# Variance by tile, modulation rows through ScalarE and TensorE, and five norm groups without a shift column, in an adaLN block on one core

## The chip, the cores and the metric

The kernel runs on one NeuronCore of a Trainium2 chip. The core has a matrix engine (TensorE, "PE" in the profile, with its weight loads as "PEld"), a vector engine (VectorE, "DVE"), an engine for activations (ScalarE, "ACT"), a general engine (GpSimd, "POOL"), and a queue engine that issues transfers (SyncE, "SP"). Each engine works through its own list of instructions in order, and semaphores make one wait for another.

The metric is the time of one execution on the device in microseconds (us), as the median of several runs. The kernel before takes 201.45 us, the median of three runs that lie between 201.2 and 201.52 us.

## The reference

One block with adaptive layer norms: x is 2048 x 512 (bf16), c is one condition row, and six modulation rows of 512 are taken from it.

```python
def _layernorm(x, axis=-1, eps=1e-05):
    m = jnp.mean(x, axis=axis, keepdims=True)
    v = jnp.var(x, axis=axis, keepdims=True)
    return (x - m) / jnp.sqrt(v + eps)
...
    mod = (_silu(c) @ w_mod).reshape(c.shape[0], 6, 1, -1)
    sa, ca, ga, sb, cb, gb = (mod[:, 0].copy(), ...)
    h = _layernorm(x, axis=-1) * (1 + ca) + sa
    x = x + ga * _A_ref(h, A_wqkv, A_wo)
    h = _layernorm(x, axis=-1) * (1 + cb) + sb
    x = x + gb * _B_ref(h, B_w1, B_b1, B_w2, B_b2)
    return x
```

`_A_ref` is an attention with 32 heads of 16 in which each position sees 8 positions at distances 0, 2, ... 14 behind it. `_B_ref` takes a third layer norm of its input and then an MLP over the tokens: 2048 tokens to 1792 hidden values with a gelu, and back to 2048. So there are three layer norms, called norm 0, 1 and 2 in the code (`l`), and `n1_`, `n2_`, `h3_` in the names of the operations.

## The kernel before

**Tiles and chunks.** The 2048 positions are 16 tiles of 128 rows. Five chunks of 2, 4, 4, 4 and 2 tiles (`SIZES`) go through norm 0, the projections to queries, keys and values, the attention, the output projection, norm 1 with its modulation, and norm 2. The token MLP begins with the tiles that are ready and fills TensorE between the attention's operations; from the last chunk on it has TensorE for itself.

**Order.** Each operation is put into a graph with a name and an engine or a choice of engines. The order in which they are issued is a list written out by hand, `ORDER` (line 191). A letter behind a colon chooses the engine (`a` ScalarE, `d` VectorE, `p` GpSimd, `s` SyncE). Each engine runs its part of the list in that order. Six PSUM buffers (`ps`) and four large SBUF buffers (`big`) are given out while the list is walked through; an operation with `alloc` takes one and the operation with `frees` gives it back, so an evacuation that comes late holds back the matmul that wants its buffer. `fill` entries are matmuls without use.

**A norm's operations.** For each tile, sums or statistics; then for a group of tiles the variance, then `ln_rstd` (line 405): `rstd...`, a logarithm and an exponential on ScalarE that give the column `rs` = 1/sqrt(var + eps), and `nb...`, one small VectorE operation that gives the shift column `nb` = -mean x `rs`. `ln_norm` (line 420) normalizes each tile as x `rs` + `nb`, on ScalarE, VectorE or GpSimd. The name after `nb` and `rstd` is the norm's number counted from one, and the chunk (norm 0) or the first tile of the group (norms 1 and 2): `nb1_0` and `nb1_1` belong to the first two chunks of norm 0, `nb3_2` to the group of tiles 2 and 3 of norm 2.

**Norm 1's variance.** For tiles 0 to 13 ScalarE or VectorE leave two sums for each tile in `sums`: of x, and 512 times the sum of the squares. The operation `ln2m...` makes from them a scaled negative variance in `mv`, for a group of tiles at once: groups begin at tiles 0, 2, 4, 6, 10 and 12 and have two tiles, the one that begins at 6 has four (`GRP`). It is two VectorE operations, of which the second reads the first one's result.

**The modulation rows.** `build_mod_rows` (line 570) multiplies the row silu(c) with columns of `w_mod`, in two parts: `modrow0` makes the row ga, `modrow1` the rows sb, cb and gb. A matmul with a 32 times repeated column of silu(c) fills one quarter of the partitions, so four stand side by side. `mrows0` and `mrows1` evacuate PSUM into `mrows`, `st_row...` stores them to memory and `ld_row...` loads them spread over all partitions (`rows_bc`). In `mrows1` VectorE copies three rows and then writes 1 + cb over the second. `aff...` applies the rows to a normalized tile.

**Attention, as far as the prediction speaks of it.** For each chunk VectorE forms products of queries and keys (`qk...`, big from `q_sb`, `k_f`), TensorE adds them up in `psL` (`red...`), VectorE takes the maximum (`max...`, tile `m`), ScalarE the exponentials (`exp...`, `lsb` from `psL`); later VectorE multiplies weights and values (`pv...`, big from `a2sb`, `vD`) and TensorE adds these up (`pvacc...`). `ev...` are the evacuations of the projections.

Of the kernel before, what the change touches and what calls it, by code (L numbers as in the profile page):

```python
# [192 lines left out]
fill:40 ln1s1:a ln1s0:d ln1v1 ld_x_2_8 ln1v0 ln1s4:d ld_wqkv0 rstd1_0 ln1s2:a nb1_0 n1_1:d n1_0:p modcols1 tr0_0  # L193
ln1s5:d ln1v4 ln1v5 ln1v3 ln1v2 rstd1_1 nb1_1 ld_x_2_6 a1col n1_2:d n1_5:d ln1s8:a wsc0_3:p n1_4:d hT0_1:a hT0_3:a
n1_3:d hT0_0:a fill:20 hT0_2:a ld_wqkv1 ld_wmod0 ln1s9:d ld_x_3_10 ln1s6:d tr1_0 tr1_2 hT1_2:a ln1v6 qkv0_02 ln1v9
hT1_0:a qkv0_12 qkv0_10 ln1s7:d ln1v7 ln1v8 rstd1_2 hT1_3:d wsc1_0:a ev0_12:a modcols0 sab:a ld_x_3_12 nb1_2 n1_8:a
qkv0_00 qvb0 wsc0_0:p ev0_10:a ld_b2 ld_wo1 hT1_1:d qkv1_00 ln1s11:d ln1s10:d ln1s13:d qkv1_10:q ln1v11 ln1v10
qvb_cp0:a ev0_00:a ln1s12:a ev0_02:d qkv1_13 ld_wqkv2 qkv0_20 ln1v13 qk0_3 qk0_2 ev1_13:a qk0_0 qvb1 ln1v12 qkv0_22:q
ld_wrow0 red0_0 ev1_00:a qkv1_03:q ev1_10:a qk0_1 red0_1 red0_2 red0_3 mask qvb_cp1:a ev0_20:a ev0_22:a wsc1_2:p
halo_v1:a qk1_0 ev1_03:a wsc1_3:a qkv1_11:q ld_wmod2 wsc2_3:a modrow0 ld_b1 mrows0:a ev1_11:a ld_wrow2 qkv1_02 max0  # L200
wsc0_2:p ld_wo0 n1_7:p sub0 rstd1_3 qkv1_01 ld_wo2 exp0 qkv1_12:q wsc1_1:p esum0:q qk1_3 red1_0 ev1_01:a qk1_1
ev1_02:a biascols n1_6:p ld_wrow1 rcp0 smB0 ev1_12:a ld_x_4_14 ln1s14:a qkv1_22 qk1_2 a2_0_2:a xt6 ld_wrow3 modrow1
red1_1 a2_0_1:a n1_9:p wsc2_0:d ln1s15:a ln1v14 nb1_3 n1_11:a qkv1_23:q mrows1 qkv1_21 ev1_21:a red1_2 red1_3 xt8
ev1_23:a fill:1 n1_10:p qkv1_20 ev1_20:a ev1_22:a qkv2_13 qkv2_10 wsc0_1:p vd0_2 ev2_13:a ln1v15 vd0_1 max1 sub1
qkv2_00 exp1 a2_0_0:s a2_0_3:s pv0_1 vd0_0 pv0_0 st_row0 pv0_2 qkv2_03 esum1:q ld_wo3 pvacc0_0 vd0_3 halo_v2:p
biascols_cp:a pvacc0_1 pv0_3 pvacc0_2 pvacc0_3 ev2_10:a ev2_00:a qk2_0 n1_13:a n1_12:a ld_row0 woq_s rcp1 smB1
oev0_2:a qkv2_11 qkv2_02:q ev2_03:a qk2_3 qkv2_01:q red2_0 oev0_0:a wo0:q wsc2_1:a wsc2_2:a qkv2_12 ev2_11:a ev2_01:a
ev2_02:a ev2_12:a wo1 qkv2_21:q a2_1_1:a qkv2_22 x1_1:a ln2q1:a x1_0:a xt10 ln2q0:a qk2_1 qkv2_23 xt12 qk2_2 a2_1_0:s
halo_k3:a ln2m0 vd1_2 a2_1_2:s qkv3_12 a2_1_3:s pv1_2 rstd1_4 red2_1 nb1_4 vd1_0 st_row1 red2_2 red2_3 rstd2_0
ev2_22:a nb2_0 ev2_21:a qkv3_13:q ev3_13:a max2 vd1_3 pv1_0 n1_14:a vd1_1 pvacc1_2 n1_15:a qkv2_20:q ev2_20:a sub2  # L210
qkv3_22:q ev3_12:a pv1_1 qkv3_10 exp2 ev2_23:a halo_v3:a qkv3_20 n2_0:a oev1_2:a ev3_10:a esum2 rcp2 qkv3_00 ev3_22:a
qkv3_02:q ev3_00:a pv1_3 ev3_02:a pvacc1_0 ev3_20:a qkv3_01:q ev3_01:a qkv3_11:q xt14 ld_row1 n2_1:p vd2_3 pvacc1_1
smB2 aff0 qk3_0 vd2_1 fill:1 vd2_0 oev1_0:a oev1_1:a pvacc1_3 ev3_11:a qk3_1 qkv3_23:q oev1_3:a a2_2_2:s ln3s1:a
qkv3_03:q wo4 a2_2_1:s qk3_2 a2_2_0:s ev3_03:a ev3_23:a x1_4:a ln2q4:a wo2 x1_2:a a2_2_3:s red3_0 wo3:q x1_3:a ln2q3:a
qkv3_21:q ev3_21:a wo5 red3_1 pv2_3 x1_5:a vd2_2 qk3_3 qkv4_20:q red3_2 qkv4_22 red3_3 qkv4_12 fill:18 ln2q5:a
ld_w1_0_512 ln2q2:a ln2m2 pv2_0 pvacc2_0 vd3_0 ev4_20:a ln3s0:a ln3v0 ev4_12:a rstd2_2 ev4_22:a ln3v1 qkv4_02 oev2_0:a
ln2m4 rstd2_4 nb2_2 n2_2:a max3 sub3:q exp3 pvacc2_3 oev2_3:a qkv4_10:q pv2_2 vd3_2 esum3 nb2_4 pv2_1 vd3_1 n2_3:p
ld_w1_0_0 n2_5:a rcp3 smB3 pvacc2_2 fill:14 a2_3_0:s a2_3_1:s a2_3_3:s n2_4:a qkv4_00:q oev2_2:a rstd3_0 aff2 pvacc2_1
oev2_1:a wo6 wo9 wo7 aff4 nb3_0 ln3s2:d ev4_02:a ln3s3:a ln3v3 h3_1:p wo8 a2_3_2:s ev4_00:a ln3v2 ld_w2_0 ln3s4:d
rstd3_2 nb3_2 x1_9:a ln3s5:a h3_0:p mlp1_0_6_0:q x1_7:a ln3v4 x1_8:a h3_3:d mlp1_0_1_0 h3_2:d mlp1_0_6_2 mlp1_0_1_2  # L220
pv3_1 mlp1_0_5_0:q ln3v5 ev4_10:a ld_w1_0_896 x1_6:a mlp1_0_3_0:q mlp1_0_3_2:q ln2q7:a pvacc3_1 rstd3_4 mlp1_0_5_2:q
oev3_1:a mlp1_0_2_0:q pv3_0 mlp1_0_2_2:q nb3_4 h3_4:a mlp1_0_0_0:q mlp1_0_0_2 h3_5:a mlp1_0_0_4:q qk4_0 ln2q8:a
ln2q6:a park0_0:a ln2q9:a mlp1_0_6_4:q mlp1_0_2_4:q mlp1_0_1_4:q park0_1:a pv3_2 mlp1_0_5_4:q vd3_3 pvacc3_0 oev3_0:a
mlp1_0_3_4:q ld_w2_1 park0_2:a pv3_3 red4_0 ln2m6 pvacc3_2 oev3_2:a mlp1_0_4_0:q qk4_1 pvacc3_3 ld_w1_0_1152
mlp1_0_4_2:q mlp1_0_4_4:q rstd2_6 oev3_3:a wo12:q halo_v4:p vd4_2 vd4_3 nb2_6 n2_9:a qk4_2 n2_7:d qk4_3 wo10:qn red4_1
ld_w1_0_1408 n2_6:a vd4_1 n2_8:a aff6 red4_2 red4_3 max4 park0_3:a ln3s8:d ln3s6:d x1_12:a ln3v8 wo11 vd4_0 ln3s9:d
mlp1_0_7_0 ld_w2_3 park0_4:a ln3v6 mlp1_0_7_2 park0_5:a ln3v9 x1_11:a ln2q12:a mlp1_0_8_0 mlp1_0_8_2 park0_6:a wo13:n
ln3s7:a ln3v7 sub4 mlp1_0_10_0 mlp1_0_9_0 x1_13:d exp4 rstd3_6 nb3_6 esum4 mlp1_0_8_4 ln2q13:a ln2m12 mlp1_0_10_2
mlp1_0_10_4 mlp1_0_9_2 rcp4 mlp1_0_7_4 h3_8:d rstd2_12 mlp1_0_12_0 mlp1_0_12_2 mlp1_0_12_4 smB4 a2_4_1:a a2_4_0:s
mlp1_0_9_4 a2_4_2:s h3_9:d a2_4_3:a h3_7:d nb2_12 h3_6:p mlp1_0_7_6 ln2q11:a park0_7:a x1_10:d mlp1_0_8_6 ld_w1_0_1664  # L230
ln2q10:a park0_8:a n2_13:p mlp1_0_9_6 park0_9:a n2_12:d aff12 ln2m10 rstd2_10 mlp1_0_10_6 park0_10:a ln3s13:a pv4_2
nb2_10 ld_w1_1_0 pv4_1 mlp1_0_11_0 mlp1_0_11_2 mlp1_0_11_4 mlp1_0_12_6 pv4_0 mlp1_0_11_6 ld_w1_1_640 inj1_6:qn pv4_3
pvacc4_0 pvacc4_1 n2_11:a mlp1_0_13_0:q pvacc4_2 pvacc4_3 n2_10:a mlp1_0_13_2:q park0_11:a mlp1_0_13_4 oev4_0:a
oev4_2:a aff10 ln3s10:a wo14 inj1_3:n ln3s11:d ln3v11 x1_14 ln2s14 wo15 x1_15 mlp1_0_13_6 ln2v14 ln3s12:a ln3v10
ln2s15 rstd2_14 nb2_14 ln2v15 n2_14:d rstd3_10 aff14 rstd2_15 nb2_15 inj1_4:qn ln3v13 park0_12:a mlp1_1_3_6 park0_13:a
mlp1_1_6_6 inj1_1:n mlp1_1_1_6 n2_15:p mlp1_1_4_6 inj1_0:n mlp1_1_0_6 nb3_10 h3_10:a mlp1_1_4_10 mlp1_1_3_10 ln3s14:d
ld_w2_4 mlp1_1_0_10 ln3v14 ln3v12 rstd3_12 h3_11:a mlp1_1_6_10 inj1_5:n mlp1_1_5_6 mlp1_1_5_10 rstd3_14 mlp1_1_1_10
aff15 nb3_12 ln3s15:d ln3v15 h3_12:p nb3_14 park1_0:+ h3_13:p rstd3_15 nb3_15 inj1_2:n mlp1_1_2_6 ld_w1_1_896 h3_14:p
h3_15:a ld_w1_2_0 park1_1:+ mlp1_1_2_10 park1_2:+ mlp1_1_7_10 park1_3:+ park1_4:+ park1_5:+ mlp1_1_8_10 mlp1_1_10_10
park1_6:+ padd1_7 padd1_10 gelu10 padd1_8 mlp1_1_9_10 padd1_9 gelu9 mlp1_2_4_11 mlp1_2_4_14 mlp1_2_1_11 mlp1_2_1_14  # L240
padd2_1 padd2_4 gelu7 mlp1_2_0_11 mlp1_2_0_14 padd2_0 gelu0 mlp1_2_2_11 gelu4 gelu8 mlp1_2_2_14 ld_w1_1_1408
mlp1_2_3_11 mlp1_2_3_14 padd2_3 gelu3 ld_w1_2_640 mlp1_2_6_11 padd2_6 gelu6 padd2_2 gelu2 mlp1_2_5_11 mlp1_1_11_10
padd1_11 mlp1_2_5_14 padd2_5 gelu1 gelu11 mlp1_1_12_10 ld_w2_5 ld_w2_7 mlp1_1_13_10 gelu5 mlp2_0_0 padd1_12 gelu12
mlp2_0_0b ld_w2_2 ld_w2_9 ld_w2_13 ld_w2_11 padd1_13 gelu13 mlp2_0_0c mlp2_6_0 mlp2_4_0 gsc fin0_0 st_out0_0 fin4_0
st_out4_0 mlp2_8_0 fin8_0 mlp2_3_0 fin3_0 mlp2_2_0 fin2_0 st_out2_0 mlp2_1_0 fin1_0 mlp2_7_0 st_out3_0 fin6_0
st_out6_0 fin7_0 mlp2_10_0 fin10_0 st_out7_0 mlp2_11_0 mlp2_5_0 st_out1_0 fin5_0 st_out5_0 mlp2_14_0 fin11_0
# [829 lines left out]
```

## Time and profile before

| | |
|---|---|
| median of the runs | 201.45 us |
| runs | 201.52, 201.45, 201.2 us |
| span of the profiled execution, first to last instruction | 199.0 us |
| median less span | 2.45 us |
| granted clock of TensorE | 1.000 |
| transfers | 35.95 MB at 181 GB/s on average |

The profile shows one execution. Its own total time is not on the page, so its span is set against the median of the runs; what lies around the span is their difference.

A row of the timeline gives the start in us from the start of the span, the length, the engine, the line, the operation, the tile written and the tiles read, their shapes, and the count of merged instructions; in brackets is how long the engine had been idle, and what released it. Instructions of one engine overlap at their ends, so what an operation adds to its engine's list is read from the start of one to the start of the next, and not from its length. Nearly all instructions have the line 142, that of the helper which records them; they are told apart by their tiles. In the chain of waits each piece is what the end of the kernel hung on in that stretch.

### The profile page before, as it was taken

What the parts mean: (1) busy time and instruction counts of PE and PEld (TensorE: products, weight loads), DVE (VectorE), ACT (ScalarE), POOL (GpSimd) and SP (SyncE); (2) the same over time, 40 slices, a digit from 0 to 9 for tenths busy, and PEclk for the clock granted to TensorE, in tenths of its full rate; (3) what the DMA queues carried; (4) which work ended last, traced back from release to release, by engine and by line L of the source; (5) the groups of instructions that cost most, each with busy time, mean ns of one, the idle gap of its engine ahead of it and who ended that gap; (6) DMA issues with size and microseconds to landing.
All of it is one profiled execution on the core that took longest, in us unless ns stands there. A gap on an engine that the chain in (4) does not pass through costs nothing.

```text
span 199.0 us, 4560 instructions
## 1 busy us (share of the span) xinstructions
PE 189.6 (95%) x1812; PEld 95.0 (48%) x1830; DVE 159.8 (80%) x242; ACT 127.8 (64%) x305; POOL 18.7 (9%) x45
## 2 busy tenths in 40 slices
...
GB/s 159 334 355 356 192 284 90 156 53 245 243 203 293 245 182 158 152 151 303 55 308 243 49 209 160 163 215 229 335 231 311 85 14 53 28 51 56 171 53 53
DMA packets 53889, 35.95 MB, mean 181 GB/s; under 512 B 24428, under 2 KB 50668, under 8 KB 53868
## 3 DMA queue, kind: packets, MB, share of 16 engines
...
q10 hardware_dynamic: 1640, 0.46, 0.9%
q8 instruction: 14, 0.23, 0.5%
q14 instruction: 7, 0.06, 0.1%
...
## 4 chain that ended last, share of the span: by engine, by line
PE 69%; DVE 22%; issue 4%; DMA 2%; ACT 2%; DVEq 0%; ACTq 0%
PE psS L142 66%; DVE big L142 14%; DVE h L142 3%; PE psL L142 3%; DMA xx<-in_A_x_dram 2%; DVE st L142 2%; DVE mv L142 1%; ACT h L142 1%; DVE lsb L142 1%; DVE m L142 1%; DVE nb L142 1%; ACT lv L142 0%; DVE woq L142 0%; ACT rs L142 0%; ACT rb L142 0%
## 5 line engine op out<-in xcount | busy, mean ns | idle before, releaser
L142 PEld LDWEIGHTS <-wst 128*128 128x128 bf16 (+1 forms) x536 | 34.9, 101 | 34.1 <-issue 4.0
L142 PE MATMUL psS<-h,wst 128*128 128x512 bf16 (+1 forms) x333 | 50.3, 379 | 0.5 <-issue 0.3
L142 DVE TENSOR_TENSOR big<-q_sb,k_f 128x4096 bf16<-128x4096 bf16 (+1 forms) x20 | 36.6, 1860 | 0.4 <-ACT q_sb L142 0.4
L142 DVE TENSOR_TENSOR big<-a2sb,vD 128x4096 bf16<-128x4096 bf16 (+1 forms) x20 | 36.6, 1862 | 0.2
L142 DVE SCALAR_TENSOR_TENSOR h<-psS,bcol,rows_bc 128x512 f32<-128x512 f32 (+2 forms) x17 | 12.1, 711 | 22.1 <-PE psS L142 20.6
L142 PE MATMUL psS<-hT,w_qkv 128*32 128x512 bf16 (+3 forms) x360 | 29.7, 345 | 0.0
L142 PEld LDWEIGHTS <-w_qkv 128*32 128x32 bf16 (+1 forms) x402 | 19.4, 108 | 17.8 <-issue 4.4
L142 PE MATMUL psS<-gT,big 128*128 128x512 bf16 x110 | 24.7, 379 | 0.1
L142 PEld LDWEIGHTS <-big 128*128 128x128 bf16 x144 | 12.1, 98 | 13.8 <-DMA big<-in_w_mod_dram 0.6
L142 ACT ACTIVATE junk<-xx 128x512 bf16<-128x512 bf16 x26 | 16.4, 629 | 3.4 <-DVE xx L142 1.4
L142 PE MATMUL psS<-woq,o_sb 128*32 128x512 bf16 (+1 forms) x107 | 15.7, 379 | 0.9 <-ACT o_sb L142 0.6
L142 ACT ACTIVATE gT<-psS,bcol 128x512 bf16<-128x512 f32 x14 | 9.0, 686 | 8.1 <-DVE psS L142 8.0
L142 POOL TENSOR_SCALAR h<-xx,rs,nb 128x512 bf16<-128x512 bf16 x9 | 7.1, 785 | 73.3 <-DVE nb L142 34.4
L142 DVE TENSOR_TENSOR psS<-psS,gT 128x512 f32<-128x512 f32 x14 | 9.3, 696 | 5.0 <-PE psS L142 5.0
L142 PE MATMUL psS<-hT,wst 128*32 128x512 bf16 (+2 forms) x110 | 12.0, 352 | 0.1
L142 ACT ACTIVATE h<-xx,nb,rs 128x512 bf16<-128x512 bf16 x15 | 11.6, 809 | 0.3 <-DVE nb L142 0.2
L142 DVE TENSOR_TENSOR h<-h,xx 128x512 bf16<-128x512 f32 (+2 forms) x17 | 11.1, 652 | 0.6
L142 DVE BATCH_NORM_STATS2 st<-xx 128x6 f32<-128x512 bf16 x12 | 8.0, 683 | 4.3 <-DMA xx<-in_A_x_dram 4.0
L142 DVE TENSOR_TENSOR h<-h,rows_bc 128x1024 bf16<-128x1024 bf16 (+2 forms) x16 | 11.0, 690 | 0.4
L142 ACT ACTIVATE v_sb<-psS,qvb 128x512 bf16<-128x512 f32 (+1 forms) x20 | 11.0, 595 | 0.0
L142 ACT ACTIVATE q_sb<-psS,qvb 128x512 bf16<-128x512 f32 (+1 forms) x18 | 10.4, 614 | 0.3 <-PE psS L142 0.3
L142 PEld LDWEIGHTS <-ident 128*32 128x32 bf16 (+1 forms) x131 | 6.2, 101 | 9.0 <-issue 4.5
...
## 6 DMA issues: line engine op xcount, KB each, us to landing
...
```

What stands on the lines that cost most here:

```text
L142: r = fn(*a, **k)
```

## The change

It has three parts, and the list `ORDER` is the same but for what they force.

1. `ln2m`: one scalar-tensor-tensor operation for each tile, (sum x sum) - 512 x (sum of squares), instead of two tensor-tensor operations for the group.
2. `mrows1`: the 1 in 1 + cb is added in PSUM by four more matmuls in `modrow1`, with a column of ones against the identity; the evacuation is then one plain copy of 384 columns, on ScalarE, at the same place of the list. GpSimd sets the column of ones at the start.
3. `NONB`: for five groups (`1_0`, `1_1`, `3_2`, `3_12`, `3_14`) there is no `nb` operation. Their tiles are normalized as (x - mean) x `rs`, which VectorE and GpSimd do with two columns as before; none of them is normalized on ScalarE in either kernel.

```diff
+    NONB=("1_0", "1_1", "3_2", "3_12", "3_14"),
...
+    ones = T([P, 1], BF, "ones")
...
         add("act", 0.54, fa, reads=reads + ["ident", "act_table"], writes=[("rs", l, g0)], name="rstd" + name)
+        if name in NONB:
+            return
...
-        G.add_any([("act", 0.8, lambda: nc.scalar.activation(dst, src, ACT.Identity, scale=r_, bias=n_)),
-                   ("dve", 0.42, lambda: nc.vector.tensor_scalar(dst, src, r_, n_, op0=ALU.mult, op1=ALU.add)),
-                   ("pool", 0.8, lambda: nc.gpsimd.tensor_scalar(dst, src, r_, n_, op0=ALU.mult, op1=ALU.add))],
-                  reads=reads + [("rs", l, g0), ("nb", l, g0)], writes=writes, name=name, locks=True)
+        sv, so = ((r_, n_), (ALU.mult, ALU.add))
+        nonb = f"{l + 1}_{g0 if l else T0.index(g0)}" in NONB
+        if nonb:
+            sv, so = (ln_t["mv", l][:, st, 0:1], r_), (ALU.subtract, ALU.mult)
+        G.add_any(([] if nonb else [("act", 0.8, lambda: nc.scalar.activation(dst, src, ACT.Identity, scale=r_, bias=n_))]) +
+                  [("dve", 0.42, lambda: nc.vector.tensor_scalar(dst, src, *sv, op0=so[0], op1=so[1])),
+                   ("pool", 0.8, lambda: nc.gpsimd.tensor_scalar(dst, src, *sv, op0=so[0], op1=so[1]))],
...
+        nc.gpsimd.memset(ones[:], 1.0)
...
-                                             rhs=w_[:, kt, dt_ * P:(dt_ + 1) * P], start=(kt == 0), stop=(kt == KT - 1),
+                                             rhs=w_[:, kt, dt_ * P:(dt_ + 1) * P], start=(kt == 0),
+                                             stop=(kt == KT - 1 and (r0, r) != (1, 1)),
                                              tile_position=(0, 32 * dt_))
+                    if (r0, r) == (1, 1):
+                        for dt_ in range(KT):
+                            nc.tensor.matmul(ps(s_)[32 * dt_:32 * dt_ + 32, r * P:(r + 1) * P],
+                                             lhsT=ones[:, 0:1].to_broadcast([P, 32]), rhs=ident[:], start=False, stop=True,
+                                             tile_position=(0, 32 * dt_))
...
-            if nr == 1:
-                copy2(rows, src_, P, False, [], [("mrows", b_)], f"mrows{b_}", frees=s_)
-            else:
-                def f_cp(rows=rows, src_=src_):
-                    nc.vector.tensor_copy(rows, src_())
-                    nc.vector.tensor_scalar_add(rows[:, 1, :], src_()[:, 1, :], 1.0)
-                add("dve", 0.8, f_cp, writes=[("mrows", b_)], frees=s_, name=f"mrows{b_}")
+            copy2(rows, src_, nr * P, False, [], [("mrows", b_)], f"mrows{b_}", frees=s_)
...
-                    gs = slice(g0, g0 + gn)
-                    if gn == 1:
-                        nc.vector.scalar_tensor_tensor(mv[:, g0, 1:2], sums[:, g0, 0:1], sums[:, g0, 0:1], sums[:, g0, 1:2],
+                    for st in range(g0, g0 + gn):
+                        nc.vector.scalar_tensor_tensor(mv[:, st, 1:2], sums[:, st, 0:1], sums[:, st, 0:1], sums[:, st, 1:2],
                                                        op0=ALU.mult, op1=ALU.subtract)
-                        return
-                    nc.vector.tensor_tensor(mv[:, gs, 0], sums[:, gs, 0], sums[:, gs, 0], op=ALU.mult)
-                    nc.vector.tensor_tensor(mv[:, gs, 1], mv[:, gs, 0], sums[:, gs, 1], op=ALU.subtract)
```

In `ORDER` the five `nb` entries are left out and `mrows1` becomes `mrows1:a`.

More of the change, by code (lines that the diff above doesn't have):

```diff
@@ L192 @@
 ident ld_x_1_2:a halo0 ld_c consts ld_x1:s ld_x0:s ld_x_1_4:s act_table ln1s3:d fill:4 cps ld_wmod1 silu_exp silu_dve
[L193 to L246, printed above, removed]
@@ L247 @@
-st_out10_0 st_out11_0 ld_w2_15 fpre mlp2_9_0 mlp2_13_0 fin14_0 st_out14_0 st_out8_0 mlp2_12_0 fin9_0 st_out9_0 fin13_0
-st_out13_0 mlp2_15_0 fin12_0 st_out12_0 fin15_0 st_out15_0 mlp2_15_1 fin15_1 st_out15_1 mlp2_15_2 fin15_2 st_out15_2
+fill:40 ln1s1:a ln1s0:d ln1v1 ld_x_2_8 ln1v0 ln1s4:d ld_wqkv0 rstd1_0 ln1s2:a n1_1:d n1_0:p modcols1 tr0_0 ln1s5:d
+ln1v4 ln1v5 ln1v3 ln1v2 rstd1_1 ld_x_2_6 a1col n1_2:d n1_5:d ln1s8:a wsc0_3:p n1_4:d hT0_1:a hT0_3:a n1_3:d hT0_0:a
+fill:20 hT0_2:a ld_wqkv1 ld_wmod0 ln1s9:d ld_x_3_10 ln1s6:d tr1_0 tr1_2 hT1_2:a ln1v6 qkv0_02 ln1v9 hT1_0:a qkv0_12
@@ new lines @@
+n1_7:p sub0 rstd1_3 qkv1_01 ld_wo2 exp0 qkv1_12:q wsc1_1:p esum0:q qk1_3 red1_0 ev1_01:a qk1_1 ev1_02:a biascols n1_6:p
+ld_wrow1 rcp0 smB0 ev1_12:a ld_x_4_14 ln1s14:a qkv1_22 qk1_2 a2_0_2:a xt6 ld_wrow3 modrow1 red1_1 a2_0_1:a n1_9:p
+wsc2_0:d ln1s15:a ln1v14 nb1_3 n1_11:a qkv1_23:q mrows1:a qkv1_21 ev1_21:a red1_2 red1_3 xt8 ev1_23:a fill:1 n1_10:p
+qkv1_20 ev1_20:a ev1_22:a qkv2_13 qkv2_10 wsc0_1:p vd0_2 ev2_13:a ln1v15 vd0_1 max1 sub1 qkv2_00 exp1 a2_0_0:s a2_0_3:s
+pv0_1 vd0_0 pv0_0 st_row0 pv0_2 qkv2_03 esum1:q ld_wo3 pvacc0_0 vd0_3 halo_v2:p biascols_cp:a pvacc0_1 pv0_3 pvacc0_2
@@ new lines @@
+halo_v3:a qkv3_20 n2_0:a oev1_2:a ev3_10:a esum2 rcp2 qkv3_00 ev3_22:a qkv3_02:q ev3_00:a pv1_3 ev3_02:a pvacc1_0
+ev3_20:a qkv3_01:q ev3_01:a qkv3_11:q xt14 ld_row1 n2_1:p vd2_3 pvacc1_1 smB2 aff0 qk3_0 vd2_1 fill:1 vd2_0 oev1_0:a
+oev1_1:a pvacc1_3 ev3_11:a qk3_1 qkv3_23:q oev1_3:a a2_2_2:s ln3s1:a qkv3_03:q wo4 a2_2_1:s qk3_2 a2_2_0:s ev3_03:a
+ev3_23:a x1_4:a ln2q4:a wo2 x1_2:a a2_2_3:s red3_0 wo3:q x1_3:a ln2q3:a qkv3_21:q ev3_21:a wo5 red3_1 pv2_3 x1_5:a
+vd2_2 qk3_3 qkv4_20:q red3_2 qkv4_22 red3_3 qkv4_12 fill:18 ln2q5:a ld_w1_0_512 ln2q2:a ln2m2 pv2_0 pvacc2_0 vd3_0
@@ new lines @@
+ev4_20:a ln3s0:a ln3v0 ev4_12:a rstd2_2 ev4_22:a ln3v1 qkv4_02 oev2_0:a ln2m4 rstd2_4 nb2_2 n2_2:a max3 sub3:q exp3
+pvacc2_3 oev2_3:a qkv4_10:q pv2_2 vd3_2 esum3 nb2_4 pv2_1 vd3_1 n2_3:p ld_w1_0_0 n2_5:a rcp3 smB3 pvacc2_2 fill:14
+a2_3_0:s a2_3_1:s a2_3_3:s n2_4:a qkv4_00:q oev2_2:a rstd3_0 aff2 pvacc2_1 oev2_1:a wo6 wo9 wo7 aff4 nb3_0 ln3s2:d
+ev4_02:a ln3s3:a ln3v3 h3_1:p wo8 a2_3_2:s ev4_00:a ln3v2 ld_w2_0 ln3s4:d rstd3_2 x1_9:a ln3s5:a h3_0:p mlp1_0_6_0:q
+x1_7:a ln3v4 x1_8:a h3_3:d mlp1_0_1_0 h3_2:d mlp1_0_6_2 mlp1_0_1_2 pv3_1 mlp1_0_5_0:q ln3v5 ev4_10:a ld_w1_0_896 x1_6:a
@@ new lines @@
+park0_3:a ln3s8:d ln3s6:d x1_12:a ln3v8 wo11 vd4_0 ln3s9:d mlp1_0_7_0 ld_w2_3 park0_4:a ln3v6 mlp1_0_7_2 park0_5:a
+ln3v9 x1_11:a ln2q12:a mlp1_0_8_0 mlp1_0_8_2 park0_6:a wo13:n ln3s7:a ln3v7 sub4 mlp1_0_10_0 mlp1_0_9_0 x1_13:d exp4
+rstd3_6 nb3_6 esum4 mlp1_0_8_4 ln2q13:a ln2m12 mlp1_0_10_2 mlp1_0_10_4 mlp1_0_9_2 rcp4 mlp1_0_7_4 h3_8:d rstd2_12
+mlp1_0_12_0 mlp1_0_12_2 mlp1_0_12_4 smB4 a2_4_1:a a2_4_0:s mlp1_0_9_4 a2_4_2:s h3_9:d a2_4_3:a h3_7:d nb2_12 h3_6:p
+mlp1_0_7_6 ln2q11:a park0_7:a x1_10:d mlp1_0_8_6 ld_w1_0_1664 ln2q10:a park0_8:a n2_13:p mlp1_0_9_6 park0_9:a n2_12:d
@@ new lines @@
+aff12 ln2m10 rstd2_10 mlp1_0_10_6 park0_10:a ln3s13:a pv4_2 nb2_10 ld_w1_1_0 pv4_1 mlp1_0_11_0 mlp1_0_11_2 mlp1_0_11_4
+mlp1_0_12_6 pv4_0 mlp1_0_11_6 ld_w1_1_640 inj1_6:qn pv4_3 pvacc4_0 pvacc4_1 n2_11:a mlp1_0_13_0:q pvacc4_2 pvacc4_3
+n2_10:a mlp1_0_13_2:q park0_11:a mlp1_0_13_4 oev4_0:a oev4_2:a aff10 ln3s10:a wo14 inj1_3:n ln3s11:d ln3v11 x1_14
+ln2s14 wo15 x1_15 mlp1_0_13_6 ln2v14 ln3s12:a ln3v10 ln2s15 rstd2_14 nb2_14 ln2v15 n2_14:d rstd3_10 aff14 rstd2_15
+nb2_15 inj1_4:qn ln3v13 park0_12:a mlp1_1_3_6 park0_13:a mlp1_1_6_6 inj1_1:n mlp1_1_1_6 n2_15:p mlp1_1_4_6 inj1_0:n
@@ L249 @@
+fin5_0 st_out5_0 mlp2_14_0 fin11_0 st_out10_0 st_out11_0 ld_w2_15 fpre mlp2_9_0 mlp2_13_0 fin14_0 st_out14_0 st_out8_0
+mlp2_12_0 fin9_0 st_out9_0 fin13_0 st_out13_0 mlp2_15_0 fin12_0 st_out12_0 fin15_0 st_out15_0 mlp2_15_1 fin15_1
+st_out15_1 mlp2_15_2 fin15_2 st_out15_2
 """
@@ L581, in f_mm @@
                                              lhsT=sc[:, kt:kt + 1].to_broadcast([P, 32]),
-                                             rhs=w_[:, kt, dt_ * P:(dt_ + 1) * P], start=(kt == 0), stop=(kt == KT - 1),
+                                             rhs=w_[:, kt, dt_ * P:(dt_ + 1) * P], start=(kt == 0),
+                                             stop=(kt == KT - 1 and (r0, r) != (1, 1)),
                                              tile_position=(0, 32 * dt_))
-            add("pe", 0.3 * nr, f_mm, reads=["sc", "gT_use"] + ([("wst", 1)] if r0 == 0 else [("rowA", i) for i in range(KT)]),
+                    if (r0, r) == (1, 1):
[3 more added lines that the diff above has]
+                                             tile_position=(0, 32 * dt_))
+            add("pe", 0.3 * nr, f_mm, reads=["sc", "gT_use", "consts", "ident"] + ([("wst", 1)] if r0 == 0 else [("rowA", i) for i in range(KT)]),
                 alloc=s_, name=f"modrow{b_}", tiled=True)
```

29 lines of the change are left out of this document (28 added, 1 removed).

## The prediction

> **What bounds the kernel now.** I read the page's busy times first, then the chain of waits in order of time, and then the waits of TensorE.
>
> ```profile
> span 199.0 us, 4560 instructions
> PE 189.6 (95%) x1812; PEld 95.0 (48%) x1830; DVE 159.8 (80%) x242; ACT 127.8 (64%) x305; POOL 18.7 (9%) x45
> ```
>
> TensorE is busy for 95% of the span, so the most that faster vector work can bring lies in TensorE's few waits. The chain (start, length, engine and tile) shows whose turn it is.
>
> ```profile
> 10.60 5.81 PE psS L142 x79
> ...
> 36.83 4.16 PE psS L142 x76
> ...
> 50.56 2.31 DVE big L142
> ...
> 67.96 5.71 DVE big L142 x3
> ```
>
> The reader is to see turns: PE from 10.60 to 41, DVE to 52.9 (50.56 is its last piece), PE to 67.96, DVE again to 102.8, and then PE to the end, the token MLP. Time saved on DVE counts only in DVE's turns, and only as far as PE waits where a turn ends. These are those two waits, from the timeline of PE:
>
> ```profile
> 52.90 0.61 PE L142 MATMUL psS<-big,group 128*32 128x512 bf16 x8 [0.53 <-DVE big L142]
> 102.79 0.40 PE L142 MATMUL psL<-big,group 128*32 128x512 bf16 x4 [0.29 <-DVE big L142]
> ```
>
> So after 102.79 all later DVE and POOL savings of this change (`ln2m10`, `ln2m12`, `nb3_12`, `nb3_14`) are worth nothing: PE computes through, and they only make operands ready sooner.
>
> **Part 1, the first two norm groups lose their shift column (`nb1_0`, `nb1_1`).** The second one, its neighbours, and what PE meets next:
>
> ```profile
> 8.96 0.17 DVE L142 SCALAR_TENSOR_TENSOR nb<-mv,rs 128x4 f32<-128x4 f32 x1 [0.60 <-ACT rs L142]
> 9.04 0.16 DVE L142 TENSOR_SCALAR a1col<-psS 128x4 f32<-128x4 f32 x1
> 9.16 1.39 DVE L142 TENSOR_SCALAR h<-xx,rs,nb 128x512 bf16<-128x512 bf16 x4
> ...
> 12.68 0.36 PEld L142 LDWEIGHTS <-wst 128*128 128x128 bf16 x4 [0.15 <-DMA wst<-in_A_wqkv_dram]
> ```
>
> Without it `a1col` can start at 8.96 and the four normalizations at 9.04 instead of 9.16: 0.12 us sooner, into PE's turn at 10.60. But at 12.68 PE waits for projection weights from memory, whose load hangs on no norm. This gain, and whatever `nb1_0` gives ahead of it, ends in that wait: 0, with bounds 0 and -0.12 (if the weights land sooner in the timed runs). The `ones` column costs one more memset of one column on POOL, which idles afterwards:
>
> ```profile
> 7.02 0.91 POOL L142 TENSOR_SCALAR h<-xx,rs,nb 128x512 bf16<-128x512 bf16 x1 [3.77 <-DVE nb L142]
> ```
>
> That idle of 3.77 us is its cover; it costs nothing.
>
> **Part 2, the modulation rows `mrows1`.** DVE loses a cast and an add, ScalarE gets one evacuation of 128x384, PE gets four matmuls.
>
> ```profile
> 29.53 0.85 PE L142 MATMUL psS<-gT,sc 128*32 128x128 bf16 x48
> 30.21 0.39 PE L142 MATMUL psL<-big,group 128*32 128x512 bf16 x4
> 32.78 0.55 DVE L142 CAST mrows<-psS 128x384 bf16<-128x384 f32 x1
> 33.73 1.21 DVE L142 TENSOR_REDUCE m<-psL 128x128 bf16<-128x1024 f32 x1
> 32.82 0.82 PE L142 MATMUL psL<-big,group 128*32 128x512 bf16 x12
> 34.51 0.81 PE L142 MATMUL psS<-hT,w_qkv 128*128 128x512 bf16 x3
> ```
>
> On PE 48 such matmuls take 0.68 us (29.53 to 30.21); four stand side by side in the column groups, so twelve steps of 0.057: **+0.06**, in PE's turn, on the path. Bounds: +0.06 and +0.23 (four in a row).
>
> On DVE the cast of 0.55 us and the shorter add behind it go, which fill most of 32.78 to 33.73, but this is PE's turn. The next DVE operation is the maximum at 33.73, and it reads `psL`, which PE finishes with the matmuls that start at 32.82 and end at 33.64. DVE would now stand waiting for them: **0**; the bound for a gain is the 0.09 between 33.64 and 33.73, which the later PE eats.
>
> On ScalarE the new evacuation stands after `n1_11`, where the value evacuations start now:
>
> ```profile
> 33.98 2.40 ACT L142 ACTIVATE v_sb<-psS,qvb 128x512 bf16<-128x512 f32 x4
> 46.44 0.60 ACT L142 ACTIVATE xx<-psS 128x512 bf16<-128x512 f32 x1 [0.48 <-PE psS L142]
> ...
> 48.00 0.59 SPq L142 DMA_DIRECT2D scratch<-mrows  x1
> ```
>
> Four of 512 columns take 2.40, one 0.60; 384 columns in proportion 0.45, and with some fixed cost I take 0.49 us. It pushes what is queued behind it (four value evacuations, a key evacuation, the exponentials) by that at most. It ends near 34.47 and frees its PSUM buffer for the projection that PE starts at 34.51 (34.57 with the four matmuls): just in time. What is pushed is caught up by ScalarE's idle 0.48 before 46.44. Price **0**, bounds 0 and +0.60 if one pushed evacuation has a PE operation right behind it. The rows' store on SP's queue runs at 48.00, long after either place, so no transfer moves.
>
> **Part 3, one operation per tile for the variance (`ln2m`).** Each group had two dependent tensor-tensor operations; now one scalar-tensor-tensor per tile, independent of each other. Two of the four groups in DVE's turns:
>
> ```profile
> 73.59 0.15 DVE L142 TENSOR_TENSOR mv<-sums 128x2 f32<-128x2 f32 x1
> 73.85 0.16 DVE L142 TENSOR_TENSOR mv<-mv,sums 128x2 f32<-128x2 f32 x1
> 73.95 2.29 DVE L142 TENSOR_TENSOR big<-a2sb,vD 128x4096 bf16<-128x4096 bf16 x1
> 76.16 0.34 DVE L142 SCALAR_TENSOR_TENSOR mv<-mv,st 128x1 f32<-128x1 f32 x2
> 76.42 0.16 DVE L142 TENSOR_TENSOR mv<-sums 128x2 f32<-128x2 f32 x1
> 76.61 0.16 DVE L142 TENSOR_TENSOR mv<-mv,sums 128x2 f32<-128x2 f32 x1
> 76.69 0.16 DVE L142 SCALAR_TENSOR_TENSOR nb<-sums,rs 128x2 f32<-128x2 f32 x1
> 76.76 1.22 DVE L142 TENSOR_REDUCE m<-psL 128x128 bf16<-128x1024 f32 x1
> ```
>
> The second operation of a pair starts 0.26 after the first (73.59 to 73.85), because it waits for its result; at 76.42, 0.19 after. The new operation's nearest row is the two at 76.16: same kind, same 128x1, a column as scalar, no wait between; the next operation starts at 76.42, so each takes s = 0.13. Bounds: 0.07 (the `nb` operation, 76.69 to 76.76, with a constant for the scalar) and 0.21 (no overlap: the two last 0.34 together with 0.13 between their starts, so one alone 0.21). I take 0.13. The groups, from first start to the next other operation's start: tiles 0-1 stand in front of the chain's piece at 50.56 with waits on transfers behind them, so there only the second operation's start counts, 0.26 becomes s: -0.13. Tiles 2-3, 0.36 becomes 2s: -0.10. Tiles 4-5, 0.27 becomes 2s: -0.01. Tiles 6-9 have four operations for the old two:
>
> ```profile
> 98.50 0.17 DVE L142 TENSOR_TENSOR mv<-sums 128x4 f32<-128x4 f32 x1
> 98.77 0.17 DVE L142 TENSOR_TENSOR mv<-mv,sums 128x4 f32<-128x4 f32 x1
> 98.85 1.22 DVE L142 TENSOR_TENSOR big<-q_sb,k_f 128x2048 bf16<-128x2048 bf16 x1
> ```
>
> 0.35 becomes 4s = 0.52: **+0.17**. The multiplication after tiles 0-1 gets one more wait, since the removed one no longer implies it; I put 0.03 on that. Sum of the part: -0.04.
>
> The Trainium skill weighs against this part: "VectorE: DVE Perf Modes", section "Rules for kernel authors", advises to lower the count of chained operations and not the semaphores between them. By it two for two would gain nothing and four for two would lose. The rows disagree with its first half: 0.26 with the wait against 0.13 without it.
>
> **Part 4, `nb3_2` goes**, in DVE's turn:
>
> ```profile
> 87.42 0.25 DVE L142 SCALAR_TENSOR_TENSOR nb<-mv,rs 128x2 f32<-128x2 f32 x1
> 87.60 0.17 DVE L142 BATCH_NORM_AGGREGATE mv<-st 128x2 f32<-128x6 f32 x1
> ```
>
> The aggregate stands 0.17 sooner, and the two normalizations behind it too: **-0.17**; bounds -0.25 and -0.07 (the step of other `nb` operations). The normalizations themselves read two columns as before and cost the same.
>
> **Sum:** +0.06 - 0.04 - 0.17 = -0.15 us. In s: 9s - 1.24 for part 3, with the rest 9s - 1.32; zero at s = 0.147. The span of 199.0 becomes 198.85. Outside it the median has 201.45 - 199.0 = 2.45 us that nothing touches, so the forecast is 201.3 (runs shown: 201.2 to 201.52).
>
> **Rivals.**
>
> *Faster:* s nearer to the `nb` operation's 0.07. 9s - 1.32 is -0.42 at 0.10 and -0.69 at 0.07, but PE can only take back what it waits: 0.29 at 102.79, and about 0.1 more because it is itself let go earlier at 52.90; -0.42, so 201.03; with the head's 0.12, 200.9. For it speaks that the new operations write nothing that the next one reads; against it the 0.13 at 76.16, which are also independent.
>
> *Slower:* the operations do not overlap, s = 0.21. Place: the four before 98.85, with three score products of the last chunk queued behind them on DVE, for the last of which PE waits at 102.79. It decides from s = 0.147. 9 x 0.21 - 1.32 = +0.57, so 202.0. For it speaks that each reads a fresh scalar column written by ScalarE; against it again 76.16.
>
> *Cost goes by the count of operations:* three groups come out even, tiles 6-9 pay double (+0.35), with -0.17 and +0.06 it is +0.24, so 201.7. The rows with 0.26 and 0.13 speak against it. This is the result that the Trainium skill's rule above would give.
>
> **How the numbers follow.** A kernel of this kind can be told from no change at about 0.2%, 0.4 us: below 201.05 is faster, above 201.85 slower. Forecast 0.41 and the count rival 0.05 lie within: same 0.46. Faster 0.32. Slower 0.22, more than the rows of s alone would leave it, because ScalarE frees its buffer at 34.5 with hardly any margin. The range reaches from the faster rival with the head's gain and a little beyond, 200.75, to the slower one, 202.0; the likeliest case alone is 201.05 to 201.6 (s of 0.10 to 0.16).
>
> **What would show it.** In the profile after: normalizations sooner at 9.0 yet a weight load still waiting for `wst` near 12.7; the maximum still near 33.75 with DVE idle before it; four value evacuations 0.4 later; variance operations 0.13 apart; PE's wait near 102.7 shorter by some 0.15. What would make the prediction wrong: a PE wait on ScalarE at 34.5, variance operations 0.07 or 0.2 apart, or a PE wait in the last turn.

## The result and the profile after

| | before | after |
|---|---|---|
| median of the runs, 4 each | 201.37 us | 204.19 us |
| runs | 201.52, 201.45, 201.2, 201.28 | 203.53, 204.05, 204.34, 205.22 |
| profiled execution, time | not on its page | 203.53 us |
| profiled execution, span | 199.0 us | 201.4 us |

The ratio is 1.0151 with a 95% interval of [1.0124, 1.0178]: the kernel became slower by 2.5 to 3.6 us, outside the range of the forecast. The page's busy times after:

```profile
span 201.4 us, 4584 instructions
PE 190.5 (95%) x1834; PEld 95.0 (47%) x1834; DVE 159.2 (79%) x237; ACT 127.6 (63%) x306; POOL 24.7 (12%) x46
```

The number that moved most is that of GpSimd (POOL): it was busy for 18.7 us and is now busy for 24.7, with one small instruction more (the column of ones). The groups of GpSimd's instructions by shape (busy us, mean ns of one, then the idle time ahead of them) show which ones, first before, then after:

```profile
L142 POOL TENSOR_SCALAR h<-xx,rs,nb 128x512 bf16<-128x512 bf16 x9 | 7.1, 785 | 73.3 <-DVE nb L142 34.4 <-PE psS L142 23.1 <-ACT junk L142 15.8
L142 POOL TENSOR_SCALAR h<-h,rs,nb 128x512 bf16<-128x512 bf16 x6 | 4.6, 772 | 30.5 <-DVE nb L142 30.5
```

```profile
L142 POOL TENSOR_SCALAR h<-h,mv,rs 128x512 bf16<-128x512 bf16 x3 | 6.2, 2069 | 0.9 <-ACT rs L142 0.9
L142 POOL TENSOR_SCALAR h<-xx,rs,nb 128x512 bf16<-128x512 bf16 x8 | 6.1, 766 | 68.4 <-DVE nb L142 29.2 <-issue 23.0 <-ACT junk L142 16.1
...
L142 POOL TENSOR_SCALAR h<-xx,mv,rs 128x512 bf16<-128x512 bf16 x1 | 2.2, 2206 | 3.8 <-ACT rs L142 3.8
```

Four normalizations, the ones written as (x - mean) x `rs`, take 2.07 us (the one in the head 2.21) where the form x `rs` + `nb` takes 0.77. Size and types are the same. Three of the four stand in a row (tiles 12, 13 and 14). The timeline of GpSimd and PE there, before:

```profile
126.67 9.66 PE L142 MATMUL psS<-h,wst 128*128 128x512 bf16 x43
...
128.09 2.28 POOL L142 TENSOR_SCALAR h<-h,rs,nb 128x512 bf16<-128x512 bf16 x3 [1.22 <-DVE nb L142]
```

and after, with the end of the chain of waits:

```profile
126.68 4.91 PE L142 MATMUL psS<-h,wst 128*128 128x512 bf16 x22
...
127.80 6.18 POOL L142 TENSOR_SCALAR h<-h,mv,rs 128x512 bf16<-128x512 bf16 x3 [0.92 <-ACT rs L142]
...
131.98 0.38 PE L142 MATMUL psS<-h,wst 128*128 128x512 bf16 x1 [0.39 <-POOL h L142]
134.03 2.32 PE L142 MATMUL psS<-h,wst 128*128 128x512 bf16 x10 [1.68 <-POOL h L142]
```

```profile
127.80 2.07 POOL h L142
...
131.93 2.06 POOL h L142
...
134.03 64.35 PE psS L142 x325
```

Before, PE ran through without a gap. After, it stands idle for 0.39 and 1.68 us until tiles 13 and 14 are there, in the turn in which nothing can be won back. The three rows end at 133.98 in place of 130.37, 3.61 later.

The single matmuls in the trace show the margin and the loss. One group of them starts at 130.99 before and at 131.00 after, so up to there the two kernels run level. Before, its matmuls follow each other every 0.216 us; the second, third and fourth wait for GpSimd, one for each of the tiles 12, 13 and 14. So PE wants tile 14 at 131.64: there were 1.27 us of margin, and of the 3.61 us 2.34 are left, to which 0.05 come from GpSimd's end to the matmul's start. After, the matmul on tile 14 starts at 134.03 (134.035 against 131.637), 2.40 later, and from it to the start of the last matmul it is 64.11 us in place of 64.12. Thus the growth of the span, from 199.0 to 201.4, is this one wait. The idle times of 0.39 and 1.68 add up to less, 2.07, because a matmul's row is 0.38 us long while the next one starts after 0.216; by starts the two waits cost 0.55 and 1.84 us, together 2.39.

### The profile page after: what moved, and what is told of

It is laid out like the page before. It is cut to its first block, busy times and chain, and to the rows that moved or that the text cites. A ratio compares the mean times of both kernels' runs of the same rounds, so it can differ in the third digit from the quotient of the medians.

```text
span 201.4 us, 4584 instructions
## 1 busy us (share of the span) xinstructions
PE 190.5 (95%) x1834; PEld 95.0 (47%) x1834; DVE 159.2 (79%) x237; ACT 127.6 (63%) x306; POOL 24.7 (12%) x46
## 4 chain that ended last, share of the span: by engine, by line
PE 58%; issue 12%; DVE 12%; DMA 7%; POOL 4%; ACT 3%; SPq 2%; POOLq 1%; ACTq 0%; DVEq 0%
PE psS L142 55%; DVE big L142 6%; POOL h L142 4%; DMA wst<-in_B_w_dram 3%; DMA vD<-v_sb 3%; PE psL L142 2%; DVE h L142 2%; SPq L142 2%; DMA c_t<-in_c_dram 1%; POOLq L1077 1%; ACT junk L142 1%; DVE st L142 1%; DVE mv L142 1%; DVE lsb L142 1%; ACT o_sb L142 1%
## 5 line engine op out<-in xcount | busy, mean ns | idle before, releaser
L142 PE MATMUL psS<-h,wst 128*128 128x512 bf16 (+1 forms) x338 | 50.9, 379 | 2.1 <-POOL h L142 2.1
L142 PE MATMUL psS<-woq,o_sb 128*32 128x512 bf16 (+1 forms) x112 | 16.5, 379 | 0.4 <-ACT o_sb L142 0.4
L142 POOL TENSOR_SCALAR h<-xx,rs,nb 128x512 bf16<-128x512 bf16 x8 | 6.1, 766 | 68.4 <-DVE nb L142 29.2
L142 PEld LDWEIGHTS <-group 128*32 128x32 bf16 x288 | 6.8, 96 | 7.8 <-issue 3.1
```

Of the source, the lines that this page charges most:

```text
L142: r = fn(*a, **k)
```

## The experiments

Theory A: GpSimd's subtract, mult is slow, and three in a row hold PE before the last sweep. Against it stood several others: that the remaining parts cost the time, that the operands (a mean column lying two values apart) make the row slow, or that the tiles' statistics come too late.

**Shift column back for GpSimd's groups only** (on the kernel after):

```diff
-    NONB=("1_0", "1_1", "3_2", "3_12", "3_14"),
+    NONB=("1_1", "3_2"),
```

`nb1_0`, `nb3_12` and `nb3_14` return to `ORDER`.

> The kernel after, but the three groups whose tiles GpSimd normalizes (1_0, 3_12, 3_14) have their shift column back; 1_1 and 3_2, which VectorE normalizes, stay without. Theory A (GpSimd takes 2.07 us for x - mean, times rs, where it took 0.77 for x rs + nb, and three in a row hold TensorE before the last sweep of the token MLP): GpSimd's rows are 0.77 again, TensorE's wait of 1.68 us on h at 134.03 is gone, and the time is that of before plus the small terms, which at 104 us stood at 0.0: 201.1 to 201.6 us. Rival B (the 2.2 us come from the other parts: the modulation rows on ScalarE, the four matmuls with ones, the variance by tile): the time stays at 203.5 or more.

Measured: 200.71 us, ratio to before 0.9983 [0.9961, 1.0004]. GpSimd and PE at the place:

```profile
128.16 2.27 POOL L142 TENSOR_SCALAR h<-h,rs,nb 128x512 bf16<-128x512 bf16 x3 [1.23 <-DVE nb L142]
...
129.33 4.91 PE L142 MATMUL psS<-h,wst 128*128 128x512 bf16 x21
```

No wait is left, so the whole loss sits in these three groups. The median lies below the expected 201.1 to 201.6, and 0.4 us below before, which took 201.12 in these runs; whether the other parts gain anything the interval leaves open. Two of the twelve runs took 202.72 and 203.22 us.

**Only the two late groups** (on the kernel before): `NONB=("3_12", "3_14")`, nothing else of the change.

> The kernel before, with one thing of the change alone: the groups 3_12 and 3_14 have no shift column, so GpSimd normalizes tiles 12, 13 and 14 as (x - mean) rs. Theory A: three rows of 2.07 us on GpSimd from about 128, TensorE waits for h about 2.3 us before the last sweep, 203.4 to 204.0 us. Rival B (the other parts cost the time): 201.2 to 201.5 us.

Measured: 203.53 us, ratio 1.0112 [1.009, 1.0134], PE's idle times on `h` again 2.1 us together, 2.39 by starts. One of its four runs, the profiled one, took 205.13; what that one adds is told under the hardware.

**The three tiles on VectorE** (on the kernel after):

```diff
-h3_12:p ... h3_13:p ... h3_14:p
+h3_12:d ... h3_13:d ... h3_14:d
```

> The kernel after, with the normalizations of tiles 12, 13 and 14 on VectorE in place of GpSimd, the same two operations subtract and multiply. Theory A (the cost is GpSimd's alone): each takes about 0.3 to 0.4 us on VectorE, whose own work there is an aggregate and a shift column and two parked sums; the three tiles are ready by 131, TensorE does not wait, 201.0 to 201.6 us. Rival C (the pair subtract, multiply is slow on any engine, or what makes TensorE wait is the later moment at which the tiles' statistics are ready): rows of over 1 us on VectorE, or still a wait on h, over 202 us.

Measured: 201.68 us, ratio 1.0038 [1.002, 1.0056]. The timeline of VectorE, and below it two pieces of the chain of waits:

```profile
128.66 0.38 DVE L142 TENSOR_SCALAR h<-h,mv,rs 128x512 bf16<-128x512 bf16 x1
128.96 0.68 DVE L142 TENSOR_TENSOR gT<-psS,gT 128x512 bf16<-128x512 f32 x1
129.56 0.40 DVE L142 TENSOR_SCALAR h<-h,mv,rs 128x512 bf16<-128x512 bf16 x1
```

```profile
130.35 0.61 DVE gT L142
131.00 0.59 PE psS L142 x2
```

The same pair of operations takes 0.4 us on VectorE: the price belongs to GpSimd. The time is a little above the 201.0 to 201.6 that were expected, though, and part of it has a reason that no theory had put down: the three operations push the parked sums (`gT`) back on VectorE, these free PSUM buffers, and PE now waits for them. In the trace the matmul at 131.00 starts 0.45 us after its predecessor instead of 0.216, a loss of 0.24 us. The median lies 0.56 us above that of before; where the rest comes from is not shown.

**Which pairs are slow** (on the kernel before): ten of GpSimd's normalizations get other operations.

```diff
+        pair = dict(n2_1=(ALU.subtract, ALU.mult), n2_3=(ALU.mult, ALU.subtract), h3_0=(ALU.add, ALU.mult),
+                    h3_1=(ALU.mult, ALU.mult), h3_6=(ALU.subtract, ALU.mult), n2_13=(ALU.mult, ALU.subtract),
+                    n2_15=(ALU.subtract, ALU.subtract), h3_12=(ALU.add, ALU.add), h3_13=(ALU.mult, ALU.add),
+                    h3_14=(ALU.add, ALU.mult)).get(name, (ALU.mult, ALU.add))
+        sv = (ln_t["mv", l][:, st, 0:1], r_) if name == "h3_13" else (r_, n_)
```

> The kernel before with other pairs of operations in ten of GpSimd's normalizations of 128x512, so it computes other values there (its output is not the reference's): in order of time n2_1 subtract, mult; n2_3 mult, subtract; h3_1 mult, mult; h3_0 add, mult; h3_6 subtract, mult; n2_13 mult, subtract; n2_15 subtract, subtract; h3_12 add, add; h3_13 mult, add with the columns mean and rs as in the change; h3_14 add, mult. All but h3_13 read the columns rs and nb as before. Theory A1 (the pair of operations sets the time): n2_1 and h3_6 take 2.07 us although they read rs and nb, and h3_13 takes 0.77 although it reads mean and rs; the others show which pairs are quick. Theory A2 (the operands set it: a mean column with a stride of two): h3_13 alone takes 2.07, all others 0.77.

The timeline of GpSimd, in the order of the expectation:

```profile
53.39 2.08 POOL L142 TENSOR_SCALAR h<-xx,rs,nb 128x512 bf16<-128x512 bf16 x1 [14.66 <-DVE nb L142]
77.29 2.08 POOL L142 TENSOR_SCALAR h<-xx,rs,nb 128x512 bf16<-128x512 bf16 x1 [21.82 <-PE psS L142]
86.24 1.52 POOL L142 TENSOR_SCALAR h<-h,rs,nb 128x512 bf16<-128x512 bf16 x2 [6.87 <-DVE nb L142]
...
109.05 2.08 POOL L142 TENSOR_SCALAR h<-h,rs,nb 128x512 bf16<-128x512 bf16 x1 [21.10 <-DVE nb L142]
111.83 2.08 POOL L142 TENSOR_SCALAR h<-xx,rs,nb 128x512 bf16<-128x512 bf16 x1 [0.70 <-DVE nb L142]
127.18 2.08 POOL L142 TENSOR_SCALAR h<-xx,rs,nb 128x512 bf16<-128x512 bf16 x1 [13.26 <-DVE nb L142]
130.34 2.10 POOL L142 TENSOR_SCALAR h<-h,rs,nb 128x512 bf16<-128x512 bf16 x1 [1.09 <-DVE nb L142]
132.42 0.77 POOL L142 TENSOR_SCALAR h<-h,mv,rs 128x512 bf16<-128x512 bf16 x1
133.18 0.77 POOL L142 TENSOR_SCALAR h<-h,rs,nb 128x512 bf16<-128x512 bf16 x1
```

| first, second operation | us |
|---|---|
| mult, add; add, mult; mult, mult | 0.76 to 0.77 |
| subtract, mult; mult, subtract; subtract, subtract; add, add | 2.08 to 2.10 |

The row at 132.42 reads the mean and `rs` columns of the change and takes 0.77; those at 53.39 and 109.05 read `rs` and `nb` and take 2.08. So the pair sets the time and the operands do not. Any pair tried with a subtraction is slow; that add, add is slow too says that it is not the subtraction as such. What it is no run shows. The kernel's one run took 203.33 us; it also delays other tiles, so only the lengths of its rows are used here.

The Trainium skill, "GPSIMD Engine Reference", section "Elementwise — side-by-side cycle accounting", gives 768 ns predicted and 769 measured for 512 elements in its best case. The quick pairs agree with that (0.77); for the slow ones the page has no price.

**The pair turned round** (on the kernel after): the three groups keep a column, but it is the negated mean, which needs no `rs`, and GpSimd does add, mult.

```diff
+            add("dve", 0.1, lambda: nc.vector.tensor_scalar_mul(nb[:, sl, 0], mv[:, sl, 0], -1.0), reads=reads,
+                writes=[("nb", l, g0)], name="nb" + name)
...
+            sv, so = (n_, r_), (ALU.add, ALU.mult)
```

> The kernel after, but the three groups that GpSimd normalizes (1_0, 3_12, 3_14) get a column with the negated mean, one small VectorE operation ahead of the square root, and are normalized as (x + (-mean)) rs: add, mult in place of subtract, mult. Theory A (the pair of operations sets GpSimd's time, and a sum followed by a product is a quick pair): GpSimd's rows take 0.77 us again, no wait of TensorE on h before the last sweep, 200.4 to 201.4 us. Rival E (what is slow is any normalization that does the sum ahead of the product in this place, or the missing multiplication in the column): 2.07 us and 203.5 or more.

Measured: 200.99 us, ratio 0.9996 [0.9978, 1.0014], and on GpSimd:

```profile
127.61 2.40 POOL L142 TENSOR_SCALAR h<-h,nb,rs 128x512 bf16<-128x512 bf16 x3 [0.92 <-ACT rs L142]
```

The same arithmetic, at the same moment as in the kernel after (released by `rs`, 0.92 of idle ahead), with the sign moved into the column: 0.8 us a tile, and nobody waits. Rival E falls.

**One slow row in place of three** (on the kernel before): `NONB=("3_14",)`.

> The kernel before, with only the group 3_14 without its shift column: one slow row on GpSimd (tile 14) in place of three. Theory A (TensorE waits for the end of GpSimd's row of three): tile 14 starts at 129.6 and ends at 131.67 in place of 130.37, TensorE wants it at 130.99, so it waits 0.7 us: 201.7 to 202.1 us, ratio 1.003 to 1.004. Rival F (a fixed price, such as a stall of the sequence or the clock, whatever the number of slow rows): 203 or more; if slow rows did not matter: 201.2.

Measured: 201.12 us, ratio 0.9994 [0.998, 1.0008]: no loss, a miss. GpSimd's row and PE:

```profile
126.76 9.52 PE L142 MATMUL psS<-h,wst 128*128 128x512 bf16 x43
...
129.89 2.07 POOL L142 TENSOR_SCALAR h<-h,mv,rs 128x512 bf16<-128x512 bf16 x1
```

The row is slow, and PE still runs through. The expectation took 130.99, the start of the group of matmuls, for the moment at which tile 14 is wanted; it is wanted in the group's fourth matmul. (In this execution the group starts at 131.29, and GpSimd's rows lie 0.30 later than before as well.) That matmul started at 132.02, 0.06 after GpSimd's end at 131.96, and 0.294 after the one before it instead of 0.216, so 0.08 us were lost. One slow row adds 1.30 us, and the margin is 1.27: it is used up almost exactly. The loss is not proportional to the number of slow rows; it begins where their delay passes the margin. Rival F falls as well.

**The parts alone, and the change again.** On the kernel before, one part each: group `1_0` alone, the variance alone, the modulation rows alone, the groups `1_1` and `3_2` alone; and the kernel after unchanged.

> The kernel after, unchanged, timed beside the parts on one chip. Theory A (GpSimd's pair costs about 2.3 us before the last sweep and the other parts sum to about nothing): before plus 2.0 to 2.5 us, a ratio of 1.010 to 1.013. Rival D (the slow pair costs more than the last sweep shows, for instance in the head, where tile 0's normalization takes 2.2 us): before plus 3 us or more, a ratio of 1.015 as in the first comparison.

> The kernel before, with only the group 1_0 without its shift column: tile 1 is normalized on VectorE, tile 0 on GpSimd as (x - mean) rs. Theory A: GpSimd's row at 7.0 takes 2.2 us in place of 0.9, TensorE's first transposes start 0.5 us later and the loss ends in the wait for projection weights at 12.7: ratio 0.999 to 1.001. Rival D: it reaches the end, 0.5 us, a ratio of 1.002 to 1.004.

> The kernel before, with one scalar-tensor-tensor operation for each tile as the variance, nothing else. By the forecast's term: -0.04 us, ratio 0.998 to 1.001, operations 0.13 us apart. Rival (the price of the operations is the forecast's upper bound): +0.5 us, ratio 1.002 or more.

> The kernel before, with only the modulation rows through ScalarE and the four matmuls with ones. By the forecast's term: +0.06 us, ratio 0.999 to 1.001. Rival (ScalarE's queue frees buffers late): up to +0.6 us, ratio 1.003, with a wait of TensorE on ScalarE near 34.5 or 42.

> The kernel before, with only the groups 1_1 and 3_2, whose tiles VectorE normalizes, without their shift column. By the forecast's terms: 0 for 1_1 and -0.17 us for 3_2, ratio 0.998 to 1.000; VectorE's normalizations with subtract, mult as long as before (0.40 us). Rival (the pair is dearer on VectorE too): over 1.000.

| kernel | median us | ratio to before, interval | forecast's term |
|---|---|---|---|
| after again | 203.83 | 1.0147 [1.0122, 1.0171] | |
| `1_0` alone | 200.79 | 0.999 [0.9976, 1.0003] | 0 |
| variance alone | 200.92 | 0.9992 [0.9981, 1.0003] | -0.04 us = 0.9998 |
| modulation rows alone | 201.16 | 1.0 [0.9978, 1.0022] | +0.06 us = 1.0003 |
| `1_1`, `3_2` alone | 200.73 | 0.9984 [0.997, 0.9999] | -0.17 us = 0.9992 |

The intervals hold every one of the small terms, and are too wide to say more than that. The head's slow row does not reach the end. For the kernel after, the ratio lies between what theory A and rival D expected and settles nothing by itself; `1_0` alone speaks against rival D.

**Without the parts that lose** (on the kernel before): `NONB=("1_1", "3_2")`, and the variance by tile except in the group of four, which keeps its pair of operations.

> The kernel before, with the groups 1_1 and 3_2 without their shift column and the variance by tile for the groups of one and two tiles; the group of four keeps its pair of operations, and the modulation rows stay on VectorE. By the forecast's terms: -0.17 - 0.13 - 0.10 - 0.01 + 0.03 = -0.38 us, ratio 0.997 to 0.9995. Rival (TensorE's waits at 52.9 and 102.8 have other causes that take the gain back): 0.9995 to 1.001.

Measured: 200.75 us, ratio 0.9986 [0.9973, 0.9999]; the forecast's terms make 0.9981. It is below both kernels, by 0.14% against before, which is less than the 0.2% at which the forecast speaks of faster; and it is no faster than the groups `1_1` and `3_2` alone (0.9984), so what the variance adds to them is not shown.

## Why the prediction was wrong

**The step that failed** is the cost of the normalizations. The prediction speaks of it only in the last sentence of part 4: "The normalizations themselves read two columns as before and cost the same." There it stands for `nb3_2`, whose tiles are normalized on VectorE, and for these it holds (two in 0.70 us after against 0.74 before, in the rows under part 4 below). For the four tiles on GpSimd the sum has no term at all: their cost was put at nothing, and it is 1.3 us for each tile. The trace of before had no row of GpSimd with a subtraction, so the cost was unknown and should have been bounded like the others. The edit changed the operation, the prediction compared only the operands.

**"After 102.79 all later DVE and POOL savings of this change are worth nothing: PE computes through"** is right for savings, and it hid the loss. That PE computes through is a margin, of 1.27 us for tile 14, and not a property of the stage. The sentence looked at what would become ready sooner and asked of nothing whether it becomes ready later. "A PE wait in the last turn" stood among the things that would make the prediction wrong, and that is what came, though with no cause named for it.

**Part 1: the 0 came out, for reasons it did not have.** First the rows of before, then those of after:

```profile
8.76 0.61 PE L142 MATMUL psS<-ident,h 128*128 128x128 bf16 x8
...
10.60 0.84 PEld L142 LDWEIGHTS <-h 128*128 128x128 bf16 x15 [0.43 <-DVE h L142]
...
11.61 1.59 PE L142 MATMUL psS<-hT,wst 128*128 128x256 bf16 x11
```

```profile
9.14 1.06 DVE L142 TENSOR_SCALAR h<-xx,mv,rs 128x512 bf16<-128x512 bf16 x3 [0.48 <-ACT rs L142]
...
9.28 0.62 PE L142 MATMUL psS<-ident,h 128*128 128x128 bf16 x8 [0.82 <-POOL h L142]
...
11.71 1.74 PE L142 MATMUL psS<-hT,wst 128*128 128x256 bf16 x14
```

The 0.12 us that the normalizations were to start sooner did not come: VectorE's four start at 9.14 in place of 9.16, because they now wait for `rs` itself. And GpSimd's slow row in the head held PE's first transposes back, from 8.76 to 9.28. Most of these 0.52 us went into the 0.43 us that PE's weight loads had waited for VectorE's `h` at 10.60, a wait that is gone after. The projections start only 0.10 later, at 11.71 in place of 11.61, and that went into the 0.15 us of wait for `wst` at 12.68, which is gone too.

**Part 2: right.** The rows of ScalarE and VectorE after:

```profile
33.33 0.40 DVE L142 SCALAR_TENSOR_TENSOR mv<-mv,st 128x1 f32<-128x1 f32 x1 [0.53 <-ACT junk L142]
33.68 1.22 DVE L142 TENSOR_REDUCE m<-psL 128x128 bf16<-128x1024 f32 x1
...
33.90 0.47 ACT L142 ACTIVATE mrows<-psS 128x384 bf16<-128x384 f32 x1
34.27 2.41 ACT L142 ACTIVATE v_sb<-psS,qvb 128x512 bf16<-128x512 f32 x4
```

The evacuation takes 0.47 (0.49 was put down), the value evacuations start 0.29 later than at 33.98, and the maximum, at 33.68, gains 0.05 and no more from VectorE's new idle time of 0.53.

**Part 3: right in the price of an operation.** The operations of the groups after, and what follows each:

```profile
73.76 0.34 DVE L142 SCALAR_TENSOR_TENSOR mv<-sums 128x1 f32<-128x1 f32 x2
74.02 2.28 DVE L142 TENSOR_TENSOR big<-a2sb,vD 128x4096 bf16<-128x4096 bf16 x1
...
98.34 0.60 DVE L142 SCALAR_TENSOR_TENSOR mv<-sums 128x1 f32<-128x1 f32 x4
98.86 1.22 DVE L142 TENSOR_TENSOR big<-q_sb,k_f 128x2048 bf16<-128x2048 bf16 x1
```

Two in 0.26 and four in 0.52: s = 0.13, as taken. Tiles 2-3 went from 0.36 to 0.26, tiles 6-9 from 0.35 to 0.52. What the part is worth in time, its own run leaves open (0.9981 to 1.0003).

**Part 4's own term: right.** VectorE before, from the aggregate ahead of `nb3_2` to the product behind the normalizations, and after:

```profile
86.66 0.17 DVE L142 BATCH_NORM_AGGREGATE mv<-st 128x2 f32<-128x6 f32 x1
...
87.71 0.74 DVE L142 TENSOR_SCALAR h<-h,rs,nb 128x512 bf16<-128x512 bf16 x2
88.36 2.29 DVE L142 TENSOR_TENSOR big<-a2sb,vD 128x4096 bf16<-128x4096 bf16 x1
```

```profile
86.69 0.17 DVE L142 BATCH_NORM_AGGREGATE mv<-st 128x2 f32<-128x6 f32 x1
...
87.58 0.70 DVE L142 TENSOR_SCALAR h<-h,mv,rs 128x512 bf16<-128x512 bf16 x2
88.19 2.28 DVE L142 TENSOR_TENSOR big<-a2sb,vD 128x4096 bf16<-128x4096 bf16 x1
```

From 86.66 to 88.36 it was 1.70 us; from 86.69 to 88.19 it is 1.50: -0.20, where -0.17 was forecast.

**The sum of the small terms** was to be -0.15 us by the end of VectorE's last turn. In the profiled executions PE's piece there starts at 102.79 before and at 102.80 after, and the wait ahead of it is longer, not shorter:

```profile
102.80 0.40 PE L142 MATMUL psL<-big,group 128*32 128x512 bf16 x4 [0.47 <-DVE big L142]
```

The same piece starts anywhere from 102.39 to 103.48 in the profiled executions of the kernels with one part or some of them, so one execution of each can't show 0.15 us.

**What stays open.** The wait of 2.39 us fits the runs: those of the kernels with three slow rows whose granted clock was 0.998 or more lie on average 2.6 us (first comparison), 2.4 (again) and 2.3 (the late groups only) above the median of before. Why GpSimd is slow with some pairs is not shown, and neither is the worth of the small parts.
